# Attention with pooled keys and a top-128 MLP: how the probabilities are turned in even blocks, and where queries are split

## The chip, the cores and the metric

The kernel runs on one core of one Trainium2 chip. Its time is the device time of one execution in microseconds (us); lower is better. PE is TensorE's matmul, PEld its weight load, DVE is VectorE, ACT is ScalarE, POOL is GpSimd and SP is SyncE, which issues the DMAs.

## The reference

```python
B, N, C = 4, 12288, 128                       # batches, queries, width
kv_pool = kv.reshape(B, H//4, 4, W//4, 4, C).mean(axis=(2, 4))
k = v = kv_pool.reshape(B, 768, C) @ w_sr     # 768 keys a batch
s = (q @ k.T) / sqrt(C);  s -= s.max(-1)
a = exp(s) / (exp(s).sum(-1) + 1e-9)
x = a @ v                                     # attention, [B, N, C]
score = x @ w_gate                            # one number a query
top = the 128 queries of a batch with the largest score
out = x;  out[top] += sigmoid(score[top]) * (relu(x[top] @ w1) @ w2)
```

## The kernel before

**Blocks.** Each batch is worked off in 48 blocks of 256 queries (two groups of 128), 192 blocks in all; the loop at L790 counts them with `i`. Block `i` has scores of 128 partitions x 1536 columns (two groups x 768 keys) in one of two PSUM buffers, `s_flat[i % 2]`. Every matmul that needs more than 16-bit precision is split into high and low halves: a query has `qh` and `ql` (`split_q`, L368: ACT casts, POOL subtracts; one call serves two blocks), keys have `kh`, `kl`, `kb`, the probabilities a high half in fp16 and a low half in bf16, and the values `vx` a high half `vx[:, 0]` and a low half `vx[:, 1]`.

**One block.** PE computes the scores of block `i + 1` (`S_together`) while ACT takes the exponentials of block `i` (`exp`). DVE has taken the row maxima `m` before (`s_max`), as the first step of the iteration. The probabilities then have to be turned, keys onto partitions, before they can be multiplied with the values. Twelve tiles of 128 x 128 for each half are turned in two ways. Most go through a transposing DMA from `hl` to `at` (`turn`, issued on SP one block later). The last `turned(n)` tiles are turned by PE in fp32 (`turn_pe`), ahead of the split into halves, and are then split straight from PSUM by ACT and DVE (`to_high`, `to_low` with part 2; tile name `at`). For the rest ACT makes the high half (part 0, `hl<-am`) and POOL the low half.

**Shared columns.** Where `own(n)` is 256 (L429: fewer than two tiles turned, and not one of the last three blocks), the exponentials of columns 768 to 1023 stay in PSUM (part 1). ACT casts their high half from there (`hl<-s`) and DVE subtracts their low half (L828), as the second DVE step of the next iteration. Before, this is so in batch 3 alone: `turned` (L424) gives 2 for batches 0 to 2, and 0 or 1 for even and odd blocks of batch 3.

**The values.** Five blocks later (LAG) PE multiplies the turned probabilities with `vx` (`AV_parts`, L505): for each group of queries 18 matmuls, 6 of high x high, 6 of high x low and 6 of low x high, each 130 columns wide: 128 values, a column of ones (L191, it gives the sum of the row) and the column of the gate score. `sums`, `gate_scores` and `finish` (DVE) divide by the sums and write rows to `x`, which a DMA stores.

**Order of the side work.** Everything issued on an engine keeps program order (`InOrder`). The keys of the next batch (`next_keys`, L313) and the selection of the batch before (`topk`) run as generators that advance by one step at named points of an iteration. POOL's share of a key tile is seven additions, one per block at point "d", the last thing in an iteration (L899); the seventh writes `pooled`. Two blocks later, at point "pe" between the two halves of the value matmuls (L821), PE multiplies `pooled` with the weights (`project`). `split_q` stands at L836, in even blocks, ahead of the points "ev" to "g". On POOL the order is thus: low half of block `i - 1` (odd), side addition, `ql` (for blocks `i + 2` and `i + 3`), low half of block `i`.

**Queues.** All large DMAs go through SP in program order: the transposes, loads of queries, quarter loads of `kv` (256 KB) during the first 34 or so blocks of a batch, and the stores.

Of the kernel before, what the change touches and what calls it, by code (L numbers as in the profile page):

```python
# [19 lines left out]
P = 128  # L20
# [8 lines left out]
QT = 2  # L29
# [39 lines left out]
def attention_topk_mlp(ctx, tc, a, outs, capacity):  # L69
# [118 lines left out]
    def v_split(b):  # L188
        kv = kvset[b]
        mx, sg, vx, raw = (kv[k] for k in ("mx", "sg", "vx", "raw"))  # L190
        pool.memset(vx[:, 0, :, C:C + 1], 1.0)  # L191
        pool.memset(vx[:, 1, :, C:C + 1], 0.0)
        yield "pe"
        ps = small_psum([P, 2 * P], 0, "prep").rearrange("p (a b) -> p a b", a=2)
        for i in range(2):
            pe.transpose(ps[:, i], mx[:, i:i + 1].broadcast_to([P, P]), ident)
        yield "g"
        widest(ps)
        scales(sg)
        yield "d"  # L200
        vw3, col = raw[:, :, 2 * P:], slice(C + 1, VC)
        act.activation(vw3, vw3, AF.Copy, scale=sg[:, 1:2])
        act.copy(vx[:, 0, :, col], vw3)
        pool.tensor_tensor(out=vx[:, 1, :, col], in0=vw3, in1=vx[:, 0, :, col], op=ALU.subtract)
        for lo, hi in (0, 2), (2, 4), (4, KT):
            yield "d"
            while now[0] % 2:
                yield "d"
            v, h, l = raw[:, lo:hi, P:2 * P], vx[:, 0, lo:hi, 0:C], vx[:, 1, lo:hi, 0:C]
            act.activation(v, v, AF.Copy, scale=sg[:, 0:1])  # L210
            act.copy(h, v)
            pool.tensor_tensor(out=l, in0=v, in1=h, op=ALU.subtract)
        kv["ready"] = True
# [5 lines left out]
    def first_keys():  # L219
        new_keys(0)  # L220
        halves = [(h, 0, P // 2) for h in range(2)]
        pieces = {kc: halves for kc in range(KT)}
        pieces[KT - 1] = [halves[0], (1, 0, P // 4), (1, P // 4, P // 2)]
        raws = [load_kv(0, 0, 2)]
        sp.dma_start(out=w_v[:, 0:C], in_=a["w_sr"])
        sp.dma_start(out=cst[:, 3 * P:4 * P], in_=a["cst"][:, 3 * P:4 * P])
        raws += [load_kv(0, 1)]
        spare = qp.tile([P, CHUNK], F32, name="q_raw").rearrange("p (h k t) -> p h k t", h=2, t=TAPS)
        load_q(0, 0, 0, 2 * BLK)
        raws += [load_kv(0, 2)]  # L230
        for kc in range(3, KT):
            raws.append(spare if kc == 3 else kvp.tile([P, 2, P // 2, TAPS], F32, name="kv_raw"))
            for h, lo, hi in pieces[kc]:
                sp.dma_start(out=raws[kc][:, h, lo:hi], in_=a["kv"][:, 0, kc, h, lo:hi])
        for lo, hi in (0, 3 * P), (4 * P, 5 * P):
            sp.dma_start(out=cst[:, lo:hi], in_=a["cst"][:, lo:hi])
        load_q(0, 0, 2 * BLK, CHUNK)
        act.activation(w_k, w_v[:, 0:C], AF.Copy, scale=SK)
        split_q(0, 0)
        kv = kvset[0]  # L240
        for kc in range(KT):
            pooled = kvs.tile([P, P], F32, name="pooled")
            for h, lo, hi in pieces[kc]:
                dve.tensor_reduce(out=pooled[:, h * P // 2 + lo:h * P // 2 + hi], in_=raws[kc][:, h, lo:hi], axis=AX.X, op=ALU.add)
            if kc == 0:
                dve.scalar_tensor_tensor(out=prod, in0=w_v[:, 0:C], scalar=1.0, in1=wg, op0=ALU.mult, op1=ALU.mult, accum_out=w_v[:, C:C + 1])
            ps = banks[kc % 2][:, 0:2 * P + 1]
            if kc < KT - 1:
                project(pooled, ps)
                act.copy(kv["raw"][:, kc], ps)  # L250
                split_k(0, kc, kc + 1, 0)
                split_k(0, kc, kc + 1, 1)
                if 0 < kc < KT - 2:
                    warm(14, s_flat[1][:, 0:P])
            else:
                S(0, (0,))
                project(pooled, ps)
                later = S(0, (2, 4, 5, 6))
                kh, kl, kb = (kv[k][:, kc * P:(kc + 1) * P] for k in ("kh", "kl", "kb"))
                rest = kv["raw"][:, kc, 0:P]  # L260
                act.copy(kh, ps[:, 0:P])
                dve.tensor_tensor(out=rest, in0=ps[:, 0:P], in1=kh.bitcast(F32), op=ALU.subtract)
                dve.tensor_scalar(out=kl, in0=rest, scalar1=MID, scalar2=None, op0=ALU.mult)
                act.copy(kb, ps[:, 0:P])
                act.copy(kv["raw"][:, kc, P:], ps[:, P:])
                early = [first_max(0, BANK)]
                others(early[0], [r.ins for r in later])
        pool.tensor_copy(tri16, tri)
        pool.tensor_copy(ident16, ident)
        pool.memset(kv["vx"][:, 0, :, C:C + 1], 1.0)  # L270
        pool.memset(kv["vx"][:, 1, :, C:C + 1], 0.0)
        S(0, (7, 8), [r.ins for r in early])
        S(1)

    def first_values():
        kv = kvset[0]
        mx, sg, vx, raw = (kv[k] for k in ("mx", "sg", "vx", "raw"))
        yield "g"
        for pair in range(3):
            v_max(0, pair)  # L280
        v_peak(0)
        yield "pe"
        ps = banks[1][:, 0:2 * P].rearrange("p (a b) -> p a b", a=2)
        for i in range(2):
            pe.transpose(ps[:, i], mx[:, i:i + 1].broadcast_to([P, P]), ident)
        yield "g"
        widest(ps)
        scales(sg)
        yield "g"
        v, vw, col = raw[:, :, P:2 * P], raw[:, :, 2 * P:], slice(C + 1, VC)  # L290
        dve.tensor_scalar(out=vx[:, 0, :, 0:C], in0=v, scalar1=sg[:, 0:1], scalar2=None, op0=ALU.mult)
        yield "b"
        act.activation(v, v, AF.Copy, scale=sg[:, 0:1])
        act.activation(vw, vw, AF.Copy, scale=sg[:, 1:2])
        act.copy(vx[:, 0, :, col], vw)
        pool.tensor_tensor(out=vx[:, 1, :, 0:C], in0=v, in1=vx[:, 0, :, 0:C], op=ALU.subtract)
        pool.tensor_tensor(out=vx[:, 1, :, col], in0=vw, in1=vx[:, 0, :, col], op=ALU.subtract)
        kv["ready"] = True
# [121 lines left out]
    def direct(n):  # L420
        return n >= nb - NDIR

    def turned(n):
        return 2 if n < 3 * NBLK else 0 if direct(n) else n % 2  # L424

    def together(n):
        return EARLY <= n < nb - NDIR - 1
# [77 lines left out]
    def AV_parts(n, j, dest=None, apart=(), step=3 * KT):  # L505
        vx = kvset[blocks[n][0]]["vx"]
        assert kvset[blocks[n][0]].get("ready")
        ah, al = ([st[n]["at"][:, at_place(n, h, j * KT + kt)].bitcast(t) for kt in range(KT)] for h, t in enumerate((F16, BF16)))
        if j == 0:
            st[n]["o"] = o_all if dest is None else dest  # L510
        o = st[n]["o"][:, j]
        tiles = list(range(KT))
        if j and own(n):
            tiles = tiles[2:KT - turned(n)] + tiles[0:2] + tiles[KT - turned(n):]
        mm = [(ah, h, kt) for kt in range(KT) for h in range(2)] + [(al, 0, kt) for kt in range(KT)]
        for i, (w, h, kt) in enumerate(mm):
            r = pe.matmul(o, w[kt], vx[:, h, tiles[kt]], start=(i == 0), stop=(i == len(mm) - 1))
            others(r, apart)
            st[n].setdefault("av", []).append(r.ins)
            if i % step == step - 1:  # L520
                yield
# [5 lines left out]
    def sums(n):  # L527
        b, blk = blocks[n]
        o, sg = st[n]["o"], kvset[b]["sg"]
        rz = sm.tile([P, QT], F32, name="rz")  # L530
        dve.tensor_scalar(out=rz, in0=o[:, :, C], scalar1=1e-9, scalar2=sg[:, 3:4], op0=ALU.add, op1=ALU.mult)
        st[n]["rz"] = rz

    def recip(n):
# [5 lines left out]
    def gate_scores(n):  # L540
        b, blk = blocks[n]
        if b not in scores:
            scores[b] = tk.tile([P, NCOL], F32, name="sc")
        dve.tensor_tensor(out=scores[b][:, blk * QT:(blk + 1) * QT], in0=st[n]["o"][:, :, C + 1], in1=st[n]["rz"], op=ALU.mult)

    def finish(n):
        b, blk = blocks[n]
# [242 lines left out]
    for i in range(nb):  # L790
# [35 lines left out]
        if i:  # L826
            if own(i - 1):
                mine = [to_low(i - 1, 1, dve)]  # L828
                for y in side:
                    tc.declare_no_dep(mine[0], y, reason="other banks")  # L830
            turn(i - 1, (0, 1) if together(i - 1) else (1,))
        if i % 2 and i - 1 + BPC < nb:
            nb_, nblk = blocks[i - 1 + BPC]
            load_q(nb_, nblk // BPC, nblk % BPC * BLK, (nblk % BPC + 2) * BLK)
        if i % 2 == 0 and i + 2 < nb:
            split_q(*blocks[i + 2])  # L836
        InOrder.seen.clear()
        for point in ("ev", "up", "t", "cmp", "g"):
            at_point(point)
# [56 lines left out]
                f()  # L896
        if i == 0:
            warm(24, banks[0][:, 0:P])
        at_point("d")  # L899
        if old and blocks[m][1] == NBLK - 1:  # L900
            start(select, topk(blocks[m][0]))
# [269 lines left out]
```

## Time and profile before

| | |
|---|---|
| runs of the kernel before | 915.09 us median of 3 (914.81 to 917.0) |
| the profiled execution | 914.62 us, span 912.8 us |
| granted TensorE clock | 0.999 of full speed |
| busy: PE / PEld / DVE / ACT / POOL | 96 / 82 / 77 / 83 / 81% of the span |

Busy time is an average over the span, and a busy PE need not be computing at its peak. The spacing of one instruction that comes once in a block shows the time of a block, and the idle time in square brackets behind an instruction shows what its engine waited for.

### The profile page before, as it was taken

What the parts mean: (1) busy time and instruction counts of PE and PEld (TensorE: products, weight loads), DVE (VectorE), ACT (ScalarE), POOL (GpSimd) and SP (SyncE); (2) the same over time, 40 slices, a digit from 0 to 9 for tenths busy, and PEclk for the clock granted to TensorE, in tenths of its full rate; (3) what the DMA queues carried; (4) which work ended last, traced back from release to release, by engine and by line L of the source; (5) the groups of instructions that cost most, each with busy time, mean ns of one, the idle gap of its engine ahead of it and who ended that gap; (6) DMA issues with size and microseconds to landing.
All of it is one profiled execution on the core that took longest, in us unless ns stands there. A gap on an engine that the chain in (4) does not pass through costs nothing. (4 is left out here: it accounts for less than half of the span.)

```text
span 912.8 us, 25661 instructions
## 1 busy us (share of the span) xinstructions
PE 878.4 (96%) x9993; PEld 745.4 (82%) x10179; DVE 702.5 (77%) x1855; ACT 757.8 (83%) x1240; POOL 739.3 (81%) x513
## 2 busy tenths in 40 slices
PE   4999999999999999999999999999999999999987
PEld 4788888888888888888888888888888888888865
DVE  6767766777678888887767888888776888888894
ACT  2888888888988888888988888888898888988852
POOL 2798988988899889988888898999787777778721
PEclk9999999999999999999999999999999999999999
DMA  9899999999999999999999999999899999999980
GB/s 364 191 233 238 246 237 245 235 242 231 242 229 231 242 245 249 238 229 246 231 212 237 236 228 245 234 241 235 203 218 200 252 228 253 232 221 241 245 166 22
DMA packets 557882, 209.83 MB, mean 230 GB/s; under 512 B 521408, under 2 KB 522944, under 8 KB 557376
## 3 DMA queue, kind: packets, MB, share of 16 engines
q1 hardware_dynamic: 557504, 207.66, 106.7%
q8 instruction: 79, 1.29, 0.6%
q0 software_dynamic: 256, 0.52, 0.2%
q14 instruction: 43, 0.35, 0.1%
HBM read 52.04 MB, written 25.43 MB: 85 GB/s over the span
## 5 line engine op out<-in xcount | busy, mean ns | idle before, releaser
L54 POOL TENSOR_TENSOR hl<-am,hl 128x1280 bf16<-128x1280 f32 (+2 forms) x191 | 497.3, 2604 | 118.3 <-ACT hl L54 59.2
L54 PE MATMUL o_two<-vx,at 128*128 128x130 f16 x6768 | 428.0, 219 | 0.0
L54 PEld LDWEIGHTS <-at 128*128 128x128 f16 (+1 forms) x6912 | 397.9, 97 | 33.3 <-issue 31.9
L54 ACT ACTIVATE am<-s,m 128x512 f32<-128x512 f32 (+1 forms) x526 | 357.4, 707 | 33.9 <-DVE m L54 20.2
L54 DVE TENSOR_REDUCE m<-s 128x2 f32<-128x1536 f32 (+1 forms) x192 | 336.5, 1752 | 46.4 <-PE s L54 46.1
L54 PE MATMUL s<-kh,qh 128*128 128x256 f32 (+1 forms) x771 | 254.4, 407 | 0.0
L54 ACT CAST hl<-am 128x1280 f16<-128x1280 f32 (+2 forms) x191 | 239.2, 1252 | 4.6
L54 PE MATMUL s<-kl,qh 128*128 128x256 bf16 (+1 forms) x699 | 214.7, 320 | 6.0 <-POOL ql L54 2.3
L54 PE MATMUL s<-kb,ql 128*128 128x512 bf16 (+1 forms) x661 | 202.8, 316 | 6.0 <-POOL ql L54 2.1
L54 PEld LDWEIGHTS s<-kh,qh 128*128 128x128 f32 x771 | 133.0, 190 | 30.1
L54 DVE TENSOR_TENSOR at<-s,at 128x256 bf16<-128x256 f32 (+1 forms) x166 | 67.3, 405 | 83.9 <-ACT at L54 81.6
L54 POOL TENSOR_TENSOR ql<-q_raw,qh 128x512 bf16<-128x512 f32 x96 | 122.8, 1279 | 10.8 <-ACT qh L54 10.8
L54 ACT CAST at<-s 128x256 f16<-128x256 f32 (+1 forms) x166 | 59.5, 358 | 64.2 <-PE s L54 64.1
L54 PEld LDWEIGHTS <-ql 128*128 128x128 bf16 x771 | 75.0, 97 | 35.2 <-POOL ql L54 8.3
L54 PEld LDWEIGHTS <-qh 128*128 128x128 bf16 x771 | 75.1, 97 | 26.9 <-issue 3.6
L54 DVE TENSOR_TENSOR x<-o_two,rz 128x256 f32<-128x256 f32 x186 | 77.5, 416 | 0.0
L54 DVE TENSOR_SCALAR rz<-o_two,sg 128x2 f32<-128x2 f32 x187 | 40.5, 217 | 32.2 <-PE o_two L54 31.8
L54 PE MATMUL s<-cst,am 128*128 128x128 f32 x310 | 61.7, 275 | 1.3 <-ACT am L54 1.1
L54 ACT CAST qh<-q_raw 128x512 fp32r<-128x512 f32 x96 | 59.4, 619 | 3.8 <-DMA q_raw<-in_q 3.8
L54 POOL TENSOR_TENSOR kv_sum<-kv_raw 128x256 f32<-128x256 f32 x72 | 52.9, 734 | 0.0
L54 PEld LDWEIGHTS s<-cst,am 128*128 128x128 f32 x310 | 38.9, 140 | 11.6 <-ACT am L54 5.0
L54 DVE RECIPROCAL rz<-rz 128x2 f32<-128x2 f32 x189 | 31.4, 166 | 6.4
(215 smaller groups left out, 563.0 us busy)
## 6 DMA issues: line engine op xcount, KB each, us to landing
out<-x SPq DMA_DIRECT2D x94, 256.0 KB, 2.9
q_raw<-in_q SPq DMA_DIRECT2D x93, 256.0 KB, 3.5
kv_raw<-in_kv SPq DMA_DIRECT2D x70, 256.0 KB, 3.8
at<-hl SPq DMA_TRANSPOSE x200, 5.6
kv_raw<-in_kv SPq DMA_DIRECT2D x3, 1024.0 KB, 9.1
kv_raw<-in_kv SPq DMA_DIRECT2D x5, 512.0 KB, 7.0
q_raw<-in_kv SPq DMA_DIRECT2D x2, 512.0 KB, 10.2
w<-in_w SPq DMA_DIRECT2D x2, 512.0 KB, 8.0
```

The lines of the kernel that those rows point to most:

```text
L54: r = f(*args, **kwargs)
```

## The change

Six things are edited.

1. `turned(n)` gives 1 for even blocks of batches 0 to 2 and 2 for odd ones. With that `own(n)` becomes 256 in those even blocks: PE turns one tile, the DMA 22 instead of 20 (both halves counted), ACT makes the high half of columns 768 to 1023 from PSUM, and DVE their low half in the following odd iteration.
2. In the values the gate score moves from column 129 to column 128, and the ones from 128 to 129.
3. The low half of the values has no column for the ones any more; the memset that set it to 0 goes.
4. The value matmuls against the low half (`h = 1`) are 129 columns wide.
5. `split_q` moves: it is issued in odd blocks (for blocks `i + 3` and `i + 4`), at the end of the iteration and ahead of point "d".
6. The first such call (block 2) stays in iteration 0.

```diff
@@ -188,8 +188,7 @@
     def v_split(b):
         kv = kvset[b]
         mx, sg, vx, raw = (kv[k] for k in ("mx", "sg", "vx", "raw"))
-        pool.memset(vx[:, 0, :, C:C + 1], 1.0)
-        pool.memset(vx[:, 1, :, C:C + 1], 0.0)
+        pool.memset(vx[:, 0, :, C + 1:VC], 1.0)
         yield "pe"
         ps = small_psum([P, 2 * P], 0, "prep").rearrange("p (a b) -> p a b", a=2)
         for i in range(2):
@@ -198,7 +197,7 @@
         widest(ps)
         scales(sg)
         yield "d"
-        vw3, col = raw[:, :, 2 * P:], slice(C + 1, VC)
+        vw3, col = raw[:, :, 2 * P:], slice(C, C + 1)
         act.activation(vw3, vw3, AF.Copy, scale=sg[:, 1:2])
         act.copy(vx[:, 0, :, col], vw3)
         pool.tensor_tensor(out=vx[:, 1, :, col], in0=vw3, in1=vx[:, 0, :, col], op=ALU.subtract)
@@ -267,8 +266,7 @@
                 others(early[0], [r.ins for r in later])
         pool.tensor_copy(tri16, tri)
         pool.tensor_copy(ident16, ident)
-        pool.memset(kv["vx"][:, 0, :, C:C + 1], 1.0)
-        pool.memset(kv["vx"][:, 1, :, C:C + 1], 0.0)
+        pool.memset(kv["vx"][:, 0, :, C + 1:VC], 1.0)
         S(0, (7, 8), [r.ins for r in early])
         S(1)
 
@@ -287,7 +285,7 @@
         widest(ps)
         scales(sg)
         yield "g"
-        v, vw, col = raw[:, :, P:2 * P], raw[:, :, 2 * P:], slice(C + 1, VC)
+        v, vw, col = raw[:, :, P:2 * P], raw[:, :, 2 * P:], slice(C, C + 1)
         dve.tensor_scalar(out=vx[:, 0, :, 0:C], in0=v, scalar1=sg[:, 0:1], scalar2=None, op0=ALU.mult)
         yield "b"
         act.activation(v, v, AF.Copy, scale=sg[:, 0:1])
@@ -421,7 +419,7 @@
         return n >= nb - NDIR
 
     def turned(n):
-        return 2 if n < 3 * NBLK else 0 if direct(n) else n % 2
+        return 1 + n % 2 if n < 3 * NBLK else 0 if direct(n) else n % 2
 
     def together(n):
         return EARLY <= n < nb - NDIR - 1
@@ -514,7 +512,7 @@
             tiles = tiles[2:KT - turned(n)] + tiles[0:2] + tiles[KT - turned(n):]
         mm = [(ah, h, kt) for kt in range(KT) for h in range(2)] + [(al, 0, kt) for kt in range(KT)]
         for i, (w, h, kt) in enumerate(mm):
-            r = pe.matmul(o, w[kt], vx[:, h, tiles[kt]], start=(i == 0), stop=(i == len(mm) - 1))
+            r = pe.matmul(o[:, 0:VC - h], w[kt], vx[:, h, tiles[kt], 0:VC - h], start=(i == 0), stop=(i == len(mm) - 1))
             others(r, apart)
             st[n].setdefault("av", []).append(r.ins)
             if i % step == step - 1:
@@ -528,7 +526,7 @@
         b, blk = blocks[n]
         o, sg = st[n]["o"], kvset[b]["sg"]
         rz = sm.tile([P, QT], F32, name="rz")
-        dve.tensor_scalar(out=rz, in0=o[:, :, C], scalar1=1e-9, scalar2=sg[:, 3:4], op0=ALU.add, op1=ALU.mult)
+        dve.tensor_scalar(out=rz, in0=o[:, :, C + 1], scalar1=1e-9, scalar2=sg[:, 3:4], op0=ALU.add, op1=ALU.mult)
         st[n]["rz"] = rz
 
     def recip(n):
@@ -541,7 +539,7 @@
         b, blk = blocks[n]
         if b not in scores:
             scores[b] = tk.tile([P, NCOL], F32, name="sc")
-        dve.tensor_tensor(out=scores[b][:, blk * QT:(blk + 1) * QT], in0=st[n]["o"][:, :, C + 1], in1=st[n]["rz"], op=ALU.mult)
+        dve.tensor_tensor(out=scores[b][:, blk * QT:(blk + 1) * QT], in0=st[n]["o"][:, :, C], in1=st[n]["rz"], op=ALU.mult)
 
     def finish(n):
         b, blk = blocks[n]
@@ -829,11 +827,11 @@
                 for y in side:
                     tc.declare_no_dep(mine[0], y, reason="other banks")
             turn(i - 1, (0, 1) if together(i - 1) else (1,))
+        if i == 0:
+            split_q(*blocks[2])
         if i % 2 and i - 1 + BPC < nb:
             nb_, nblk = blocks[i - 1 + BPC]
             load_q(nb_, nblk // BPC, nblk % BPC * BLK, (nblk % BPC + 2) * BLK)
-        if i % 2 == 0 and i + 2 < nb:
-            split_q(*blocks[i + 2])
         InOrder.seen.clear()
         for point in ("ev", "up", "t", "cmp", "g"):
             at_point(point)
@@ -896,6 +894,8 @@
                 f()
         if i == 0:
             warm(24, banks[0][:, 0:P])
+        if i % 2 and i + 3 < nb:
+            split_q(*blocks[i + 3])
         at_point("d")
         if old and blocks[m][1] == NBLK - 1:
             start(select, topk(blocks[m][0]))
```

## Rows read from the trace of the kernel before

**Rows 1.** Page, part 1: busy us, share of span and instructions by engine.

```profile
PE 878.4 (96%) x9993; PEld 745.4 (82%) x10179; DVE 702.5 (77%) x1855; ACT 757.8 (83%) x1240; POOL 739.3 (81%) x513
```

**Rows 2.** Timeline, PE: start, duration in us, engine, line, instruction, count.

```profile
304.47 0.38 PE L54 MATMUL s<-cst,am 128*128 128x128 f32 x2
...
304.69 0.27 PE L54 MATMUL s<-kl,qh 128*128 128x256 bf16 x1
...
305.69 1.03 PEld L54 LDWEIGHTS <-at 128*128 128x128 f16 x18 [0.16 <-issue]
```

**Rows 3.** Timeline, DVE, a plain stretch of batch 1: row maxima.

```profile
305.89 1.76 DVE L54 TENSOR_REDUCE m<-s 128x2 f32<-128x1536 f32 x1 [0.17 <-PE s L54]
...
310.21 1.76 DVE L54 TENSOR_REDUCE m<-s 128x2 f32<-128x1536 f32 x1 [0.17 <-PE s L54]
```

**Rows 4.** Timeline, DVE, batch 3: row maxima of blocks 172 to 174.

```profile
786.08 1.76 DVE L54 TENSOR_REDUCE m<-s 128x2 f32<-128x1536 f32 x1 [0.40 <-PE s L54]
...
790.19 1.76 DVE L54 TENSOR_REDUCE m<-s 128x2 f32<-128x1536 f32 x1 [0.49 <-PE s L54]
...
794.39 1.76 DVE L54 TENSOR_REDUCE m<-s 128x2 f32<-128x1536 f32 x1 [0.37 <-PE s L54]
```

**Rows 5.** Waits, whole span: total us, times, longest us.

```profile
PEld L54 <- POOL ql L54: 8.3, 17, 1.1
...
PE s L54 <- POOL ql L54: 4.4, 11, 1.0
```

**Rows 6.** Timeline, ACT, batch 1: last exponential and last cast of a block.

```profile
305.16 0.91 ACT L54 ACTIVATE am<-s,m 128x768 f32<-128x768 f32 x1
...
306.10 1.26 ACT L54 CAST hl<-am 128x1280 f16<-128x1280 f32 x1
```

**Rows 7.** Timeline, ACT, batch 3, odd block: the same two steps.

```profile
760.33 0.91 ACT L54 ACTIVATE am<-s,m 128x768 f32<-128x768 f32 x1
...
761.37 1.17 ACT L54 CAST hl<-am 128x1152 f16<-128x1152 f32 x1
```

**Rows 8.** Lines by form, DVE: count, busy us, mean ns, idle before.

```profile
L54 DVE TENSOR_TENSOR hl<-s,hl 128x256 bf16<-128x256 f32 x45 | 18.6, 414 | 0.0
```

**Rows 9.** Timeline, batch 0: a low half of queries, and PE's load of it.

```profile
81.70 1.27 POOL L54 TENSOR_TENSOR ql<-q_raw,qh 128x512 bf16<-128x512 f32 x1
...
83.02 0.10 PEld L54 LDWEIGHTS <-ql 128*128 128x128 bf16 x1 [0.53 <-POOL ql L54]
```

**Rows 10.** Timeline, batch 1: POOL around a key tile's last addition, PE's use.

```profile
298.29 2.64 POOL L54 TENSOR_TENSOR hl<-am,hl 128x1280 bf16<-128x1280 f32 x1 [0.66 <-ACT hl L54]
...
300.87 0.43 POOL L54 TENSOR_TENSOR pooled<-kv_sum 128x128 f32<-128x128 f32 x1
...
301.25 1.29 POOL L54 TENSOR_TENSOR ql<-q_raw,qh 128x512 bf16<-128x512 f32 x1
...
301.91 0.44 PE L54 MATMUL s<-pooled,w_k 128*128 128x128 f32 x2
```

**Rows 11.** Timeline, the last key tile of batch 1's preparation of batch 2.

```profile
424.40 0.44 POOL L54 TENSOR_TENSOR pooled<-kv_sum 128x128 f32<-128x128 f32 x1
...
425.84 0.44 PE L54 MATMUL s<-pooled,w_k 128*128 128x128 f32 x2
```

**Rows 12.** Timeline, SP, key loads of batch 1: first and last of nine transposes.

```profile
302.90 3.30 SPq L54 DMA_TRANSPOSE at<-hl  x1
...
337.87 3.86 SPq L54 DMA_TRANSPOSE at<-hl  x1
```

**Rows 13.** Page, part 6: transposes, their count, median us to landing.

```profile
at<-hl SPq DMA_TRANSPOSE x200, 5.6
```

**Rows 14.** Timeline, PE, late in batch 3: its first wait for the DMA.

```profile
848.30 1.03 PEld L54 LDWEIGHTS <-at 128*128 128x128 f16 x18 [0.23 <-DMA at<-hl]
```

**Rows 15.** Page, part 2: DMA packets and their sizes.

```profile
DMA packets 557882, 209.83 MB, mean 230 GB/s; under 512 B 521408, under 2 KB 522944, under 8 KB 557376
```

## The prediction

> **What bounds the kernel now.** I read the page first: TensorE (PE) is busy for 96% of the span, VectorE (DVE), ScalarE (ACT) and GpSimd (POOL) for 77 to 83% [rows 1]. A busy PE need not be the bound, so the next view was the timeline of one plain block. There the transposes, the score matmuls and the value matmuls start one behind the other with no wait: two transposes start at 304.47 and the next score matmul at 304.69, so each takes 0.11 us; 18 value matmuls fill 1.03 us, 57 ns each [rows 2]. Third, the spacing of the row maxima, one per block, gives the time of a block. In batch 1 it is 4.32 us with two tiles turned on PE [rows 3]; in batch 3 it is 4.11 us with none (an even block) and 4.20 us with one (an odd block) [rows 4]. The block's time thus follows the number of turned tiles at about 0.1 us each: PE sets the pace, and the shape that this change gives to the even blocks of batches 0 to 2 (one tile turned, 256 columns shared with DVE) already runs in batch 3. Fourth come the waits of PE inside the stream: in 17 places a weight load waits for the queries' low half `ql` from POOL [rows 5]. Last, the DMA queue, because the change sends it more.
>
> **Part 1: one turned tile less in 72 even blocks.** 72 x 0.11 us = 7.9 us less on PE, all of it on the path. From the spacings the second tile is worth 4.32 - 4.20 = 0.12 us (8.6 us), the first 0.09 us (6.5 us); I take 7.9. What it moves, engine by engine:
> - ACT gets one more cast (256 columns from PSUM), but its last cast must not end later. In batch 1 the last cast ends 306.10 + 1.26 - 305.16 = 2.20 us after the start of the last exponential [rows 6]; with the shared shape in batch 3 it is 761.37 + 1.17 - 760.33 = 2.21 us [rows 7]. Cost 0; the cover is that the extra cast overlaps the exponential; without it 0.4 us per even block.
> - DVE gets one subtraction of 0.41 us [rows 8] right behind the row maximum of every odd block. Queued behind it are the search steps and the division by the sums, and PE, whose scores of the next block overwrite those 256 columns. Batch 3 has it in every block at 4.11 and 4.20 us [rows 4], so 0; if PE had to wait for all of it, 0.4 x 72 = 30 us, which batch 3 speaks against.
> - POOL subtracts 128 columns less. That is a relief off the path: 0.
> - The transposing DMA gets 22 tiles in place of 20 in those blocks; rival D has its price.
>
> **Part 2: 129 columns against the low half.** Twelve of the 36 value matmuls of a block lose one column of 130. At 57 / 130 = 0.44 ns a column [rows 2] this is 12 x 0.44 = 5 ns, in 192 blocks 1.0 us less. No row shows a value matmul of odd width, so it may be nothing, or as much to the bad: -2 to +1; I take -1.0. The two memsets that become one are a few POOL instructions off the path: 0.
>
> **Part 3: the queries' low half ahead of side work, what goes.** Before, an even block issues `ql`, behind the side addition that closes the odd block before it. In the trace `ql` ends at 82.97, and PE's weight load leaves at 83.02, 0.53 us late [rows 9]. After the change `ql` leaves one side addition (0.4 to 1.3 us) earlier and is ready before PE asks. The weight loads wait 8.3 us in all for it, the matmuls themselves 4.4 us in 11 places [rows 5]; a weight load runs ahead, so the matmuls' figure is nearer to the loss. The longest of them, 1.0 us, I leave out: it belongs to the first blocks, whose order of work is another. Saved: 3.4 us (bounds 2 and 7).
>
> **Part 4: the same swap, what comes.** The side addition is now behind `ql`. For most additions nobody is waiting, with one exception: the last addition of a key tile, `pooled`, which PE multiplies at a fixed place, between the two halves of the value matmuls two blocks later. A key tile takes seven additions, one per block, so the last one falls in an odd block in every second tile: tiles 1, 3 and 5 of three batches, nine in all. One of them is in the rows [rows 10]: POOL waits for ACT, subtracts until 300.93, `pooled` ends at 301.30, then `ql` runs; PE multiplies at 301.91, so the slack is 0.61 us. With `ql` (1.29 us, 0.05 us of it overlapped) in front, `pooled` ends 1.24 us later; with 0.05 us from POOL's end to PE's start (as in rows 9) and with the even block before it 0.11 us shorter, PE waits 1.24 + 0.05 + 0.11 - 0.61 = 0.79 us. POOL cannot start sooner, because ACT ends the wait ahead of the subtraction. The matmul stands in PE's order, so all of it is lost. Tile 5 of batches 1 and 2 has more slack, 425.84 - 424.84 = 1.00 us [rows 11], and waits 0.40 us. Together 7 x 0.79 + 2 x 0.40 = 6.3 us more. Bounds: 0, and 9 x 1.24 = 11.2 us.
>
> **Part 5: the queue.** For the additional tiles I set 1 us (bounds 0 and 11, rival D).
>
> **The sum.** -7.9 - 1.0 - 3.4 + 6.3 + 1.0 = -5.0 us. The profiled execution took 914.62 us (span 912.8 and 1.8 around it), which gives 909.6; the median of the runs is 915.09, 0.47 above it, so I forecast a median of 910.1 us.
>
> **Rivals.**
> A is the forecast: 910.1, its own range 907 to 912.3.
> B: the new wait for `pooled` doesn't come, because POOL gets ahead. For it: POOL has 128 columns less to do in even blocks. Against it: the subtraction in question belongs to an odd block and waits for ACT [rows 10]. Time: 910.1 - 6.3 = 903.8.
> C: PE waits at all 18 key tiles. The other nine come from even blocks, where ACT has the extra cast; should the last cast be late by 0.37 us (one such cast, though rows 6 and 7 speak against it) and use up their slack, 9 x 0.37 = 3.3 us come on top: 913.4.
> D, the other side: the DMA queue becomes the bound. For it: in the stretch where keys are loaded the queue issues back to back. Eight transposes in a row take (337.87 - 302.90) / 8 = 4.37 us each [rows 12], as long as a block, and the one at 302.90 begins 2 us after POOL finished its data at 300.93 [rows 10, 12]: the queue is already behind. A transpose of 20 tiles takes 3.30 us, so two more tiles take 0.33 us, 0.165 us per block on average. Key loads last for about 34 of the 48 blocks; 34 x 0.165 = 5.6 us of delay per batch. Against it: the delay is free as long as it fits. A block's tiles are used four blocks (17 us) after they are issued, and land 5.6 us after issue [rows 13]; that leaves about 6 us beyond the usual start, and the 14 blocks without key loads can drain it. In batch 3 the queue sends 22 or 24 tiles per block, and PE first waits for it at 848.30, for 0.23 us, near the end [rows 14]. If nothing is drained, 3 x 5.6 - 6 = 10.8 us are lost: 910.1 - 1.0 + 10.8 = 919.9 us. It decides as soon as the queue's time per block exceeds PE's by more than 6 us in sum over a batch.
> Of the packets 521408 of 557882 are under 512 bytes [rows 15]. The Trainium skill, "DMA: Bandwidth & Descriptors", Specifications, gives 512 bytes as the least transfer for line rate; by that rule tiles sent to the DMA are the dearest bytes it can get, which is D. The trace agrees in part: the queue is late during the key loads, yet PE hardly waits for it.
> E: the change does what it says but half of its gain goes in small delays of D's kind, some 2 to 3 us: 912.1 to 913.1, 912.6 in the middle.
>
> **How the numbers follow.** A 0.55, B 0.12, C 0.12, D 0.11, E 0.10. Runs of this kernel cannot tell less than 0.3% from no change, so "the same" is 912.3 to 917.8. Faster: A and B, with a little taken off for A's upper edge, 0.66. Same: C, E and that edge, 0.23. Slower: D, 0.11. The likeliest case gives 910.1. The range takes in B's near end and most of C, E and the milder forms of D: 904.0 to 916.0.
>
> **What the profile after would show.** Part 1: about 238 transposes on PE in place of 310, and even blocks of batches 0 to 2 at 4.20 to 4.22 us, odd ones unchanged. Part 3: the waits for `ql` nearly gone. Part 4: nine new waits of PE for `pooled`, 0.3 to 0.9 us each; if they are missing, B is right; if there are 18, C. D: waits of PE for the transposed tiles in the second half of each batch. The forecast is wrong if even blocks stay at 4.3 us (another engine had become the bound), or if PE's waits for DMA exceed 5 us.

## The result: slower, by the DMA queue

After the change the kernel takes 923.94 us (median of five runs, 921.15 to 925.29), against 914.87 us (five runs, 914.78 to 917.0) for the kernel before on the same chip: a ratio of 1.0076, interval 1.0053 to 1.0098. The forecast was 910.1 us, in a range of 904 to 916. The profiled execution took 923.94 us, 9.3 us more than the one of before (914.62), with the same granted clock of 0.999. What happened is rival D, which had a chance of 0.11 and a time of 919.9 us.

The page of the kernel after, its parts 1 to 3 and 6 (these answer to [rows 1], [rows 15] and [rows 13]):

```profile
PE 874.5 (95%) x9930; PEld 737.4 (80%) x10107; DVE 717.8 (78%) x1927; ACT 760.1 (82%) x1312; POOL 721.8 (78%) x509
...
DMA packets 576315, 214.56 MB, mean 233 GB/s; under 512 B 539840, under 2 KB 541376, under 8 KB 575808
...
q1 hardware_dynamic: 575936, 212.38, 109.6%
...
at<-hl SPq DMA_TRANSPOSE x200, 5.8
```

PE is busy 3.9 us less in a span that is 9.3 us longer, so PE waits more. The median time to landing hardly moved (5.6 to 5.8 us) and shows nothing. `q1` is the queue that carries the transposes, loads and stores. Its packets' times add up to more than 100% of the 16 engines' span, so this share alone does not show that the queue is full. Before it was:

```profile
q1 hardware_dynamic: 557504, 207.66, 106.7%
```

The waits of the kernel after (total us, times, longest us), answering to [rows 5]; `at` are the transposed tiles, `o_two` is the output of the value matmuls:

```profile
PEld L54 <- DMA at<-hl: 18.4, 22, 2.7
...
PE o_two L54 <- DMA at<-hl: 11.4, 14, 2.4
ACT hl L54 <- DMA at<-hl: 9.0, 10, 2.3
...
PEld s L54 <- POOL pooled L54: 5.8, 9, 0.8
...
PE s L54 <- POOL pooled L54: 4.1, 8, 0.6
```

The waits for `ql` are gone but for one of 0.6 us, and the nine for `pooled` are there. For the transposed tiles PE's weight loads now wait 18.4 us in 22 places and its matmuls 11.4 us in 14, well beyond the 5 us that the prediction named as a sign of being wrong. Before, the list had no such wait of the value matmuls, and this one of the weight loads:

```profile
PEld L54 <- DMA at<-hl: 0.9, 2, 0.7
```

A plain stretch of batch 1, the row maxima on DVE, answering to [rows 3]:

```profile
307.65 1.76 DVE L54 TENSOR_REDUCE m<-s 128x2 f32<-128x1536 f32 x1 [0.17 <-PE s L54]
311.86 1.76 DVE L54 TENSOR_REDUCE m<-s 128x2 f32<-128x1536 f32 x1 [0.41 <-PE s L54]
316.18 1.76 DVE L54 TENSOR_REDUCE m<-s 128x2 f32<-128x1536 f32 x1 [0.17 <-PE s L54]
```

Blocks of 4.21 and 4.32 us alternate where before all had 4.32: the turned tile is worth what it was priced at, as long as PE doesn't wait for a tile. That doesn't last. POOL's low half, SP's issues and PE's value matmuls, 299 to 352 us into the kernel after:

```profile
332.27 2.38 POOL L54 TENSOR_TENSOR hl<-am,hl 128x1152 bf16<-128x1152 f32 x1
```

```profile
299.72 3.64 SPq L54 DMA_TRANSPOSE at<-hl  x1
...
329.28 3.70 SPq L54 DMA_TRANSPOSE at<-hl  x1
...
344.36 3.88 SPq L54 DMA_TRANSPOSE at<-hl  x1
```

```profile
351.75 1.20 PE L54 MATMUL o_two<-vx,at 128*128 128x130 f16 x18 [2.41 <-DMA at<-hl]
```

The data of block 68 are complete at 332.27 + 2.38 = 334.65, and their transpose is issued at 344.36, 9.7 us later; before, such a delay was 2.0 us [rows 10, 12]. PE then stands for 2.41 us. From 299.72 to 329.28 SP issues six transposes, one in 4.93 us, against 4.37 before [rows 12] and against the 4.21 to 4.32 of a block in which PE doesn't wait.

### The profile page after: what moved, and what is told of

Read it like the earlier page. It is cut to its first block, busy times and chain, and to the rows that moved or that the text cites. A ratio compares the mean times of both kernels' runs of the same rounds, so it can differ in the third digit from the quotient of the medians.

```text
span 922.1 us, 25669 instructions
## 1 busy us (share of the span) xinstructions
PE 874.5 (95%) x9930; PEld 737.4 (80%) x10107; DVE 717.8 (78%) x1927; ACT 760.1 (82%) x1312; POOL 721.8 (78%) x509
## 5 line engine op out<-in xcount | busy, mean ns | idle before, releaser
L54 POOL TENSOR_TENSOR hl<-am,hl 128x1280 bf16<-128x1280 f32 (+2 forms) x191 | 479.8, 2512 | 144.8 <-ACT hl L54 78.4
L54 PE MATMUL o_two<-vx,at 128*128 128x130 f16 x6768 | 427.8, 219 | 12.2 <-DMA at<-hl 11.4
L54 ACT ACTIVATE am<-s,m 128x512 f32<-128x512 f32 (+2 forms) x454 | 331.4, 747 | 35.9 <-DVE m L54 27.9
L54 ACT CAST hl<-am 128x1280 f16<-128x1280 f32 (+2 forms) x191 | 233.1, 1220 | 6.9 <-DMA at<-hl 4.6
L54 PE MATMUL s<-kl,qh 128*128 128x512 bf16 (+1 forms) x692 | 212.4, 319 | 4.2 <-DVE hl L54 2.1
L54 PE MATMUL s<-kb,ql 128*128 128x256 bf16 (+1 forms) x677 | 207.4, 317 | 4.2
L54 DVE TENSOR_TENSOR at<-s,at 128x128 bf16<-128x128 f32 (+1 forms) x166 | 57.8, 348 | 57.2 <-ACT at L54 54.6
L54 ACT CAST at<-s 128x128 f16<-128x128 f32 (+1 forms) x166 | 51.9, 312 | 52.7 <-PE s L54 48.8
L54 ACT ACTIVATE s<-s,m 128x256 f32<-128x256 f32 x117 | 52.5, 448 | 3.8
L54 PE MATMUL s<-cst,am 128*128 128x128 f32 x238 | 53.8, 275 | 1.0 <-ACT am L54 0.8
L54 DVE TENSOR_TENSOR hl<-s,hl 128x256 bf16<-128x256 f32 x117 | 48.6, 415 | 1.1 <-ACT hl L54 1.1
```

What stands on the lines that cost most here:

```text
L54: r = f(*args, **kwargs)
```

## The experiments

Three theories were tested first. Q: the queue is the bound, that is, the transposes that SP issues come too late for PE. W: the moved low halves (the new waits for `pooled`) cost more than sized. S: the shared columns themselves cost, through ACT and DVE. The expectations name them so.

**One half of the change each.** e1 is the kernel after with `split_q` back in its old place:

```diff
@@ kernel after, e1 @@
-        if i == 0:
-            split_q(*blocks[2])
...
             load_q(nb_, nblk // BPC, nblk % BPC * BLK, (nblk % BPC + 2) * BLK)
+        if i % 2 == 0 and i + 2 < nb:
+            split_q(*blocks[i + 2])
...
-        if i % 2 and i + 3 < nb:
-            split_q(*blocks[i + 3])
         at_point("d")
```

> The changed kernel with split_q back in its old place; the turned tile, the shared columns and the 129 columns stay. Theory Q (the DMA engines are full while keys load, and two more tiles in every even block push the queue so far behind that PE waits for turned tiles): PE saves 7.7 us of transposes, the waits for ql (3.7 us) come back, the nine waits for pooled (6.5 us) go, and the queue's loss of about 14 us stays or grows by some us, since PE no longer gives it time: 919 to 924 us. Rival W (the waits for pooled that the swap brings are the loss): about 908 us. Rival S (the shared columns hold up PE through DVE and ACT): 919 to 921 us, with no waits for DMA.

Measured 928.74 us (926.41 to 930.34), ratio 1.0136 (1.0112 to 1.016). Without any new wait for `pooled` it is slower than the kernel after, and slower than Q's 919 to 924; its waits:

```profile
PEld L54 <- DMA at<-hl: 26.7, 30, 1.9
...
PE o_two L54 <- DMA at<-hl: 17.3, 25, 1.6
```

W is out as the cause. e2 is the kernel before with the move of `split_q` alone (the same lines the other way round):

> The kernel before with split_q moved and nothing else. Q: nine waits for pooled of 0.7 to 0.85 us (two shorter) come, 6.5 us, and the waits for ql go, 3.7 us: 917 to 918 us, PE waits for DMA below 2 us. W: 922 us or more. S: as Q.

Measured 918.53 us (917.0 to 922.63), ratio 1.003 (1.0009 to 1.0051), some 3 us more. That agrees with parts 3 and 4 of the prediction, -3.4 + 6.3 = +2.9 us, though not cleanly, since there is a wait for the queue in it too. Its waits:

```profile
PEld s L54 <- POOL pooled L54: 5.5, 9, 0.8
...
PEld L54 <- DMA at<-hl: 3.0, 7, 0.9
```

e5 is the kernel before with the shared columns in all even blocks, and still two tiles turned on PE:

```diff
-        return OWN if turned(n) < 2 and not direct(n) else 0
+        return OWN if (turned(n) < 2 or n % 2 == 0) and not direct(n) else 0
```

> The kernel before with the shared columns in all even blocks, but still two tiles turned on PE: the DMA has 20 tiles as before, and ACT and DVE have the shared columns' extra instructions. Q: no tile is added to the queue, so 914.5 to 916.5 us. S (the shared columns hold up PE): 918 us or more, with the waits in odd blocks.

Measured 916.4 us (913.7 to 922.02), ratio 1.0008 (0.9983 to 1.0033): the additional cast on ACT and subtraction on DVE cost nothing that can be measured (0.33%, 3 us, at the upper end of the interval). S is out as the cause.

**The queue relieved.** e3 and e4 are the kernels after and before with most of the 256 KB loads of queries left out; they use the queries of the first two chunks again, so their output is not the reference's:

```diff
-            load_q(nb_, nblk // BPC, nblk % BPC * BLK, (nblk % BPC + 2) * BLK)
+            if nb_ or nblk // BPC > 1:
+                qraw[nb_, nblk // BPC] = qraw[0, nblk // BPC % 2]
+            else:
+                load_q(nb_, nblk // BPC, nblk % BPC * BLK, (nblk % BPC + 2) * BLK)
```

> The changed kernel, but the queries are loaded for the first two chunks only and used again for all others, which takes 256 KB off the DMA queue in every second block (that part of the input is left out, so the result is another). Q: the queue keeps up, PE's waits for turned tiles vanish, and 910 us are left: 923.9 less the 14 us of the queue. W and S: no less than 921 us.

> Control: the kernel before with the same loads of queries left out. Q: PE does not wait for the queue there, so 914 to 915 us, the queue only less late. W and S: the same. If it is faster by more than 2 us, the queue cost the kernel before something too.

Measured: e3 909.83 us (909.66 to 911.05), ratio 0.9932 (0.991 to 0.9953); e4 914.49 us (913.74 to 915.79), ratio 0.9982 (0.9969 to 0.9994). Less traffic is worth 14 us to the kernel after and 1 us to the one before. With the queue relieved the change gains 914.49 - 909.83 = 4.7 us, near the prediction's sum without the queue (6.0 us). The page and the waits of e3, and its SP:

```profile
q1 hardware_dynamic: 563264, 189.31, 97.3%
```

```profile
PEld s L54 <- POOL pooled L54: 7.0, 10, 0.8
...
PE s L54 <- POOL pooled L54: 5.2, 10, 0.6
```

```profile
302.73 3.35 SPq L54 DMA_TRANSPOSE at<-hl  x1
306.13 0.57 SPq L54 DMA_DIRECT2D kv_raw<-in_kv  x1
308.39 2.63 SPq L54 DMA_TRANSPOSE at<-hl  x1
```

No wait for the transposed tiles is left in the list, and SP now has free time between issues (306.70 to 308.39). Over the whole run SP's rows leave 71 us in gaps of more than 0.35 us before, 49 us after and 180 us in e3. Between 50 and 670 us from the start there are 29 such gaps before. Most of them lie at 447 to 514 us, around the first blocks of batch 2, where a block takes longer (4.79 us on average in blocks 96 to 107), and at 632 to 669 us, the last blocks of batch 2, behind the last load of keys. After, there are three, of 0.4 to 0.5 us: the pauses of the queue are gone. In e6 the low half is moved back in the nine odd blocks whose side addition writes `pooled`, on top of e3:

```diff
+        last_add = b + 1 < B and blk < 7 * KT and blk % 7 == 6
-        if i % 2 and i + 3 < nb:
+        if i % 2 and i + 3 < nb and not last_add:
             split_q(*blocks[i + 3])
         at_point("d")
+        if i % 2 and i + 3 < nb and last_add:
+            split_q(*blocks[i + 3])
```

> The kernel after, with queries loaded only for the first two chunks (their values are wrong for the rest, and 11264 packets of 2 KB are gone), and the low halves of the queries put back behind the side addition in the nine odd blocks whose addition writes pooled. With the queue relieved, part 4 stands alone against the run that only relieves the queue (909.83). Theory: the nine waits of 0.79 and 0.40 us are all lost on PE, so the time falls by 6 to 6.5 us, to 903.5 (902.5 to 904.5). Rival: PE makes the waits good elsewhere (slack of the next block): 907 to 910.

Measured 903.28 us (902.94 to 903.45), ratio 0.9871 (0.9855 to 0.9887). With the queue out of the way the nine waits are worth 909.83 - 903.28 = 6.55 us; the two ran on different chips, and by their ratios to the kernel before on each it is 5.6 us.

**PE made faster, with no packet more.** v1 is the kernel before with `split_q` moved and the same exception for the nine blocks. v2 and v4 are v1 with one tile turned in even blocks 34 to 46 of a batch, and in every fourth block:

```diff
-        return 2 if n < 3 * NBLK else 0 if direct(n) else n % 2
+        return (1 + n % 2 if n % NBLK >= 34 else 2) if n < 3 * NBLK else 0 if direct(n) else n % 2   # v2
+        return (1 if n % 4 == 0 else 2) if n < 3 * NBLK else 0 if direct(n) else n % 2               # v4
```

> The kernel before with split_q moved, except in the nine odd blocks whose side step is a key tile's last addition; there the addition stays ahead. Q and the sum of the prediction: the waits for ql go (3.4 to 3.7 us) and no wait for pooled comes: 911 to 912.5 us. If the queue is already full in the kernel before, part of that comes back as waits for DMA: 913 to 915 us.

> As v1_swap_but_last, and one tile is turned in the even blocks 34 to 46 of batches 0 to 2, where few keys are loaded (21 blocks). Q: the queue has room there, so 21 x 0.107 = 2.2 us less than v1: 909 to 910 us. If it is the blocks as such (S) and not the key loads, no gain over v1.

> As v1_swap_but_last, and one tile is turned in every fourth block of batches 0 to 2 (36 blocks, half of the change's number), key loads or not. PE saves 3.9 us against v1. Q: half of the added tiles; the queue falls behind half as fast, and PE waits for it by the end of the key loads: 910 to 917 us. If the queue's loss were proportional to the tiles (14 to 21 us for 72 blocks), 915 to 918 us.

Measured: v1 917.24 us (913.38 to 923.3), ratio 1.001 (0.9984 to 1.0037); v2 916.13 (913.32 to 920.05), 0.9998 (0.9975 to 1.0022); v4 918.47 (914.61 to 926.14), 1.0031 (1.0002 to 1.006). All three medians lie above what Q gave them (the kernel before took 915.75 us there). v1 is the sharpest of all: `ql` and `pooled` are hardly waited for any more (0.5 and 0.8 us), not one packet was added, and the time is that of before. The 3.4 us expected would be a ratio of 0.996, outside its interval. A new wait took the place of the old ones:

```profile
PEld L54 <- DMA at<-hl: 8.5, 14, 1.9
PE o_two L54 <- DMA at<-hl: 4.6, 7, 1.6
```

Its transposes start 6.4 us behind POOL's subtraction on average in blocks 24 to 35, against 1.4 us in the kernel before. That the queue has room in the late blocks of a batch (v2) was my expectation, and it was wrong. In v10 the exception is put into the kernel after:

> The kernel after with the nine low halves put back behind the additions that write pooled. With the queue relieved this was worth 6.5 us (909.83 to 903.28). Theory (the queue is the bound in the kernel after): the 6.5 us of PE's waits that go come back as waits for the queue, 921 to 925. Rival (the losses add up): 917 to 918.

Measured 926.84 us (922.35 to 931.64), ratio 1.0094 (1.0065 to 1.0123), against 1.0076 (1.0053 to 1.0098) for the kernel after: the 5.6 to 6.55 us of e6 are worth nothing here. The time is above the theory's 921 to 925, as is that of the kernel before in the same series (917.96).

```profile
PEld L54 <- DMA at<-hl: 32.6, 36, 2.9
PE o_two L54 <- DMA at<-hl: 21.3, 26, 2.6
```

**What fills the queue.** v7 (on the kernel after), v5 (on v10) and v6 (on the kernel before) load queries four blocks and keys half a tile at a time (`load_half`, a new helper), in packets of 4 KB:

```diff
-        if i % 2 and i - 1 + BPC < nb:
+        if i % 4 == 1 and i - 1 + BPC < nb:
-            load_q(nb_, nblk // BPC, nblk % BPC * BLK, (nblk % BPC + 2) * BLK)
+            load_q(nb_, nblk // BPC, nblk % BPC * BLK, (nblk % BPC + 4) * BLK)
...
-                if h in (1, 3, 5) and kc + 1 < KT:
-                    load_quarter(b, kc + 1, (h + 1) // 2, raws[kc + 1])
+                if h == 3 and kc + 1 < KT:
+                    load_half(b, kc + 1, 1, raws[kc + 1])
```

> The kernel after with the bigger loads and nothing else. Theory: half or more of the some 14 us that PE lost to the queue comes back: 913 to 919. Rival (issue of transposes is the limit): 922 to 925.

> A complete version: the kernel after, with the nine low halves put back, queries loaded four blocks at a time and keys in halves of a tile, so that these loads go in 4 KB packets in place of 2 KB ones (a 4 KB packet took 182 ns, two of 2 KB 223 ns in the trace of before: some 26 us less of the 16 engines' time in the whole run, against some 20 us that the added tiles cost). Theory (the queue's packets are the bound): 911 to 916, below the kernel before if the relief is as large as the added load. Rival (the queue is limited by the issue of transposes on SP, which bigger packets don't change): 918 to 921.

> Control: the kernel before with the same bigger loads. PE waits for the queue 0.9 us in all there, so theory and rival both say 914 to 915; only the spread of the runs may shrink. If it becomes slower, bursts of 512 KB hold up the transposes.

Measured: v7 939.55 us (932.94 to 941.54), ratio 1.0261 (1.0233 to 1.029); v5 938.24 (936.21 to 940.17), 1.025 (1.0231 to 1.0269); v6 924.62 (922.29 to 929.83), 1.0119 (1.0094 to 1.0143). All three lie above every range given: where the theory expected a gain there was a loss. The 4 KB packets took 261 ns on average in v6, more than two of 2 KB (223 ns before), and the transpose behind a large load is held up: behind a pair of loads its issue takes 5.4 us on average, 3.8 us before. SP in v6:

```profile
304.20 2.67 SPq L54 DMA_TRANSPOSE at<-hl  x1
306.92 0.57 SPq L54 DMA_DIRECT2D q_raw<-in_q  x1
307.54 0.42 SPq L54 DMA_DIRECT2D kv_raw<-in_kv  x1
308.07 5.28 SPq L54 DMA_TRANSPOSE at<-hl  x1
```

The opposite was tried as well: v8 (on v10) and v11 (on the kernel before) load queries one block at a time, 1 KB packets; v9 (on v10) keeps the 2 KB packets and loads 64 partitions at a time. Each has 92 loads more.

```diff
-        if i % 2 and i - 1 + BPC < nb:
-            nb_, nblk = blocks[i - 1 + BPC]
-            load_q(nb_, nblk // BPC, nblk % BPC * BLK, (nblk % BPC + 2) * BLK)
+        if i and i + BPC - 1 < nb:                                                    # v8, v11
+            for n in (i - 1 + BPC,):
+                nb_, nblk = blocks[n]
+                load_q(nb_, nblk // BPC, nblk % BPC * BLK, (nblk % BPC + 1) * BLK)
...
-        sp.dma_start(out=qraw[b, ch][:, lo:hi], in_=a["q"][:, b, ch, lo:hi])          # v9, in load_q
+        u, v = (0, P) if part is None else (P // 2 * part, P // 2 * part + P // 2)
+        sp.dma_start(out=qraw[b, ch][u:v, lo:hi], in_=a["q"][u:v, b, ch, lo:hi])
...
+        j = i - 1 - (i - 1) % 2 + BPC                                                 # v9
+        if i and j < nb:
+            nb_, nblk = blocks[j]
+            load_q(nb_, nblk // BPC, nblk % BPC * BLK, (nblk % BPC + 2) * BLK, (i - 1) % 2)
```

> The kernel after with the nine low halves put back, and the queries loaded one block at a time, in 1 KB packets. In the trace of before, packets of 256, 512, 1536 and 2048 bytes took 18, 27, 65 and 84 ns at the median, so about 9 ns and 37 ns per KB: two of 1 KB some 93 ns, uncontended, against 84 for one of 2 KB, 6 us more of the 16 engines' time. If size or burst makes the excess over that (27 ns a packet of 2 KB, 102 ns one of 4 KB), it shrinks: 912 to 918, below the baseline v10. If packets cost by count and bytes alone: 922 to 927.

> The same kernel with each load of queries cut in two by partitions (64 partitions an iteration), so that the packets stay at 2 KB and the burst is halved. If the length of a burst holds up the transposes: 3 us or more below the baseline v10. If packets alone count: as v10 within 1.5 us.

> The kernel before with the queries loaded one block at a time. The queue is hardly waited for there, so 914 to 916 either way; if small packets load the engines more, waits for the transposed tiles appear and it is 917 to 919.

Measured: v8 976.56 us (975.08 to 978.67), ratio 1.0651 (1.0621 to 1.0682); v9 997.46 (990.6 to 1003.65), 1.0864 (1.082 to 1.0907); v11 954.89 (948.98 to 959.7), 1.0395 (1.0356 to 1.0434). All far outside what was expected. v9 moves the same bytes in nearly the same packets; what it adds is issues on SP, and the share of `q1` falls. SP and the page of v9:

```profile
306.97 0.58 SPq L54 DMA_DIRECT2D q_raw<-in_q  x1
307.67 2.70 SPq L54 DMA_TRANSPOSE at<-hl  x1
310.41 0.59 SPq L54 DMA_DIRECT2D q_raw<-in_q  x1
311.10 0.53 SPq L54 DMA_DIRECT2D out<-x  x1
311.68 0.43 SPq L54 DMA_DIRECT2D kv_raw<-in_kv  x1
312.27 4.82 SPq L54 DMA_TRANSPOSE at<-hl  x1
```

```profile
q1 hardware_dynamic: 577408, 212.39, 101.7%
```

A load of half the size costs SP the same 0.58 us and a gap of about 0.1 us; 92 of them are some 62 us, which is of the order of what the three kernels lost against their own bases, 37 to 71 us (v11: 954.89 - 917.96; v8 and v9 against v10). So a last kernel, v12, takes v10 and issues the queries' loads from ACT:

```diff
-        sp.dma_start(out=qraw[b, ch][:, lo:hi], in_=a["q"][:, b, ch, lo:hi])
+        (sp if (b, ch) == (0, 0) else act).dma_start(out=qraw[b, ch][:, lo:hi], in_=a["q"][:, b, ch, lo:hi])
```

> The kernel after with the nine low halves put back (as v10) and the queries' loads issued from ACT in place of SP; packets and bytes are the same. In the two runs with 92 more loads the time rose by 37 us (before: 917.96 to 954.89) and 50 to 71 us (v10: 926.84 to 976.56 and 997.46), and 92 issues of 0.58 us with their gaps of 0.07 to 0.1 us are 60 to 62 us of SP. Theory now (SP's issue is the bound, the engines are filled by what it sends): 92 issues less on SP relieve it by some 60 us over the run, as the run without queries' loads did: 903 to 907, with up to 3 us for ACT's own issues if its casts come later: 903 to 910. Rival (the 16 DMA engines' time is the bound): 922 to 930, as v10.

Measured 951.68 us in the middle of six runs from 931.09 to 962.98. The runs differ too much among themselves for a ratio, but none is near the 903 to 910 that were expected if SP's issues alone were the bound. The lowest, 931.09, is as slow as v10's slowest (931.64). The page of v12, from an execution of 951.25 us:

```profile
q1 hardware_dynamic: 562688, 188.26, 101.9%
q10 hardware_dynamic: 13248, 24.12, 9.7%
```

The two queues together stand at 111.6%, no less than the 109.0% of `q1` alone in v10. The Trainium skill, "DMA: Bandwidth & Descriptors", Issuing engines are not separate DMA queues, says that transfers issued by different engines run on the same 16 DMA engines and mix there. The run is in line with that: the queries' loads issued from ACT (`q10`) left no more room for the transposes, with the share just named.

## Why the prediction was wrong, point by point

- **Part 1, -7.9 us: right.** Even blocks went from 4.32 to 4.21 us, odd ones stayed; over the plain blocks of batches 0 to 2 that is about 0.11 x 72 = 7.9 us, and e5 shows no cost of the moved work on ACT and DVE.
- **Part 2, -1.0 us: nothing.** In blocks 156 to 175 of batch 3, where the number of turned tiles is the same in both kernels and PE doesn't wait for one, the row maxima are 4.158 us apart on average before and after; 5 ns less would be 4.153. Its bounds (-2 to +1) held it.
- **Part 3, -3.4 us: right as far as can be seen.** All waits for `ql` but one of 0.6 us are gone. No run measures the gain by itself. What e2 gained and lost (+2.9) less part 4 as measured below leaves -2.7 to -3.7 us. And e6 against e4, both with the queue relieved, has parts 1 and 3 together at 914.49 - 903.28 = 11.2 us (10.2 by the ratios); the prediction had 11.3.
- **Part 4, +6.3 us: right in mechanism and size.** Nine waits came, and e6 against e3 puts them at 5.6 to 6.55 us. One of them in the kernel after, on PE:

```profile
370.65 0.49 PE L54 MATMUL s<-pooled,w_k 128*128 128x128 f32 x2 [0.62 <-POOL pooled L54]
```

- **Part 5, +1.0 us: the step that failed.** Without it the sum was -6.0 us, and e3 against e4 measured -4.7 us, the rest of the change with the queue relieved. With the queue the profiled execution is 9.3 us over, so the queue's term is 9.3 + 4.7 = 14 us; e3 says the same (923.94 - 909.83 = 14.1), although it takes more off the queue than the change had added.

Rival D had the mechanism and priced it at 10.8 us. Two of its premises, by which it was given so small a chance, did not hold. The first is that only the additional tiles load the queue, 0.165 us a block. In the stretch shown above the spacing of the transposes grew by 4.93 - 4.37 = 0.56 us. A faster PE also asks for the same tiles sooner, and v1 shows that this alone is enough: PE's waits for `ql` gone, no tile added, nothing gained. The rows held a sign of it: a transpose every 4.37 us beside a block of 4.32 us [rows 3, 12] is a queue without reserve. And the tiles are indeed dear: in the trace of before packets of 256 bytes took 18 ns at the median and those of 2 KB 84 ns, so a byte in the small ones took 1.7 times as long.

The second is the 6 us that the delay may reach, to be drained in the 14 blocks without key loads. The 6 us do not follow from the numbers beside them (17 - 5.6 is 11.4), yet they are near what the trace of after gives: at block 68 a delay of 9.7 us cost 2.41, so 7.3 were free, 5.3 beyond the usual 2.0. It is the draining that failed. Of batches 0 to 2 only the last has such a pause. In batches 0 and 1 the kernel loads a quarter of a key tile of the batch after next in blocks 40, 42, 44 and 46 (L802), so that in batch 1 of the trace of before the pause between loads of `kv_raw` lasts from 390.47 to 415.27 us, six blocks.

The delay shows it, taken as each transpose's start less the end of POOL's subtraction. In the kernel after its mean is 5.2 us in blocks 12 to 23 and 6.6 in blocks 24 to 35 (1.4 before). In the pause of batch 1, blocks 82 to 88, it falls from 10.0 to 4.8 us and no further, and only behind the last key load, in blocks 132 to 142, does it fall from 7.3 to 0. With the added tiles in the last 14 blocks of a batch alone (v2) it was 7.1 us in blocks 84 to 95, without them (v1) 4.4. So the slack is used up in batch 0, where the value matmuls wait 1.0 us for tiles, and PE pays for what comes later: 8.2 us of such waits in batch 1 and 2.2 in batch 2.

That also means that the terms do not add up once the queue is the bound. Taking 5.6 to 6.55 us of waits out of the kernel after brought nothing (v10), and e1, which lacks the +2.9 us of the moved low halves, is 4.8 us slower than the whole change. A reading that fits both is that a wait of PE gives the queue time to catch up, and that its removal is paid back as a wait for the queue.

**What stays open.** Whether SP's issues or the 16 DMA engines set the queue's rate. More issues with the same bytes slow it (v9), but fewer issues with larger packets (v6, v7), or with the same packets from another engine (v12), do not speed it up. Both may be near their limit at once; no run here separates them. Why e1 is slower than the kernel after was argued, not tested, and why v12's runs differ so much is not known. No version was found that beats the kernel before and still loads all queries.

## What to carry to other kernels

Before work is moved to a queue, or an engine that feeds on it is made faster, compare the queue's own time per step with the step: the spacing of its issues in the busiest stretch, not its median latency and not the waits that it causes. Here the queue ran at the pace of its consumer and was hardly waited for, and in v1 a saving on the consumer became a wait for it. Check also whether the pauses in which the queue is to catch up are pauses: in batches 0 and 1 they held loads for a later batch. A run with part of the queue's traffic left out, on both kernels, puts a price on it.

## What the runs showed of the hardware

- Loads of 128 KB in place of 256 KB, with the same 2 KB packets (v9), made the kernel 71 us slower than v10 (997.46 against 926.84): an issue of a load costs SP 0.58 us at either size (0.58 to 0.60 us on average in both kernels).
- Packets of 4 KB took 261 ns on average in v6, against 182 ns in the kernel before. There 1024 of the 1152 run in the first 30 us, before the stream of transposes, at 171 ns on average, and the other 128 took 270 ns: a duration read from one stretch did not carry over to another.
